# Expert blocks with gathers three blocks ahead, buffers reloaded behind their conversion, and activation splits on ScalarE and VectorE

## The chip, the cores and the metric

The kernel runs on one core of a Trainium2 chip. The metric is the device time of one execution in microseconds, the median of several runs. TensorE (PE), VectorE (DVE), ScalarE (ACT), GpSimd (POOL) and SyncE (SP) each take their own instructions in order; SP issues nearly all DMAs, POOL the indirect ones (gathers and scatters by a table of indices).

## What is computed

Three stages on 4 sequences of 768 tokens, with 384 features:

```
# 1. attention with a decaying state, 8 heads of 48
for t in range(768):
    cur = outer(u * k[t], v[t])
    y[t] = r[t] @ (state + cur)
    state = w[t][:, None] * state + outer(k[t], v[t])
# 2. dense feed-forward, 384 -> 2048 -> 384, on the 3072 tokens
h = x @ w_in
x = where(h > 0, h, exp(min(h, 0)) - 1) @ w_out
# 3. top-1 mixture of 8 experts, 384 -> 1024 -> 384
logits = x @ w_gate + modality_bias[modality_id]
e = argmax(logits); gate = softmax(logits)[e]
out = gate * (maximum(x @ w1[e], 0) @ w2[e])
```

Inputs and outputs are float32.

## The kernel before

TensorE works in float16. Every operand is held as two float16 numbers, a high half and a low half (the rest that the high half leaves), and a product is three matmuls: high by high, high by low, low by high. Making a low half is a subtraction over the whole tile, by `split` (L344) where the source is scaled, or by `lowp` (L341), whose line L342 is that subtraction on GpSimd or on VectorE:

```
def lowp(lo, f, hi, pool=True):
    (nc.gpsimd if pool else nc.vector).tensor_tensor(lo, f, hi, op=ALU.subtract)
```

**Dense groups.** The 24 tiles of 128 tokens go through the dense part in 6 groups of 4. `ffn_in` makes 16 tiles m of 9 matmuls, 512 columns each (L607); ACT's exponential (L612), two VectorE passes (L613, and L614, a maximum that reads PSUM) and an ACT copy (L615) give the high half, `lowp` the low half. `ffn_out` makes 4 token tiles of 48 matmuls, 384 columns each (L627), and `ffn_x2` stores each as two halves and transposes it by a DMA in SP's queue (L643). `logits` and `route` choose the experts. The last group has no attention beside it, but the start of the expert stage.

**Two tables.** Tokens of one expert are put together in blocks of 256. A first table (`first`, `first_b`, tag a) is made from five groups and fills the first NB = 3 blocks; a second one (`final`, `final_b`, tag b) places all that is left, and can only be made behind the last group's logits. `place_b` turns counts into index tables (idxa, idxb) by a few matmuls (L782) and nine small VectorE operations (L790 to L798). The names scr and X are the routed rows in DRAM and their source.

**Expert blocks.** There are 12 full blocks and, for these inputs, two half blocks of 128 rows, 12 and 13, counted from 0, behind branches on the numbers of blocks (`rest`, L1168 and L1173). For each block:

- `moe_gather` fetches rows by two indirect DMAs on POOL (L897) into G, one of three buffers, and SP transposes them by two DMAs (L903) into XM, also three.
- `moe_w` loads an expert's float32 weights as four quarters into four buffers (SG and, in the space of the dense weights, wi; L914, L917) and converts a quarter in two pieces, the high half by ACT (L930), the low half by VectorE (L931), into W1 and W2, two buffers each. A quarter is 768 KB.
- `moe_h` makes eight tiles of 9 matmuls, 256 columns each (128 in a half block; L939). ACT does the ReLU into mt (L945), VectorE casts it to the high half (L946), `lowp` on GpSimd makes the low half (L342).
- `moe_o` makes two token tiles of 24 matmuls, 384 columns each (one in a half block; L959): first five of the eight m for each, then the last three. VectorE scales the sum by the gate factor, which lies at the end of the gathered row in G (L966), and POOL scatters it to the output (L967).

**What sets the order.** `moe_block` issues block j's work with the loads of block j + 1 ahead of it, and the conversions of j + 1 at fixed places in it. Through `hook`, it calls the five parts of routing at ticks: the table TO gives the tick of each (`logits`, `route`, `route_b`, `final`, `final_b`), one tick for each m of `moe_h` and each step of `moe_o`, over blocks 0 and 1. A scheduler then reorders instructions within each engine, so what stands in which row is seen in the built program alone.

Of the kernel before, what the change touches and what calls it, by code (L numbers as in the profile page):

```python
# [129 lines left out]
def body(ctx, tc, r, k, v, w, u, w_in, w_out, mod, w_gate, bias, w1, w2, cst, out, dbg=None):  # L130
# [516 lines left out]
    def logits(g):
        t0, nt = GR[g]
        xt2 = xT[g]
        pt = psum("a")  # L650
        for i in range(nt):
            n = 0
            for kk in range(KD):
                for b_ in range(2):
                    for a in range(2):
                        nc.tensor.matmul(
                            pt[:, E * i:E * i + E], lhsT=xt2[:, b_ * KD + kk, 128 * i:128 * i + 128],
                            rhs=wg[:, kk, E * a:E * a + E], start=(n == 0), stop=(n == 4 * KD - 1),
                        )
                        n += 1  # L660
# [311 lines left out]
    def moe_load(j, x=True):  # L972
        e = moe_reg(j)
        moe_w(j, 0, e, 0)
        moe_w(j, 1, e, 0)
        if x:
            moe_gather(j)
        moe_w(j, 2, e, 0)
        moe_w(j, 3, e, 0)

    def moe_block(j, nxt, nt=2, x=True, hook=None, nl=True):
# [226 lines left out]
```

## Time and profile before

| | us |
|---|---|
| three runs | 894.53, 884.48, 880.47 |
| median | 884.48 |
| profiled execution | 879.89 |
| its span | 878.0 |
| TensorE busy in it | 755.0 (86%) |
| VectorE busy | 625.2 (71%) |
| GpSimd busy | 516.1 (59%) |
| ScalarE busy | 452.0 (51%) |

The profile is of one execution, the span from its first to its last instruction; 1.9 us lie outside it. The mean granted clock of TensorE is 0.955 of full speed. Lines such as L342 are lines of the kernel before. In a timeline, consecutive instructions of one kind are one row with their count, and matmuls overlap, so that a row's start minus the start of the one ahead is what it adds. In brackets stands how long the engine was idle ahead of the row and what released it: an engine with the tile and the line that it wrote.

### The profile page before, as it was taken

The numbers are of one execution on the slowest core, as the hardware profiler recorded it, in microseconds if no ns is written. First come the engines' busy times: TensorE is split into PE (matmuls) and PEld (weight loads), VectorE is DVE, ScalarE is ACT, GpSimd is POOL, SyncE is SP. The second block draws the span as 40 slices with busy tenths as digits, with TensorE's granted clock in tenths as the row PEclk, the third lists the DMA queues.
The fourth block names the chain that finished last, engine by engine and source line by source line (L and its number), as shares of the span: only waits on it lengthen the run. The fifth ranks groups of instructions, "written<-read, shape, count | busy, mean of one in ns | idle before, by whom it ended". The sixth has DMA issues, their size and how long they took to land.

```text
span 878.0 us, 17356 instructions
## 1 busy us (share of the span) xinstructions
PE 755.0 (86%) x6383; PEld 485.3 (55%) x6383; DVE 625.2 (71%) x1321; ACT 452.0 (51%) x965; POOL 516.1 (59%) x525
## 2 busy tenths in 40 slices
PE   3787575999899989998998899987997998999964
PEld 2664342665466546654665455443764765667643
DVE  5779999358965896589558951993597757776641
ACT  4675766346654565456545541462326545554431
POOL 6667778546764576467646641443255767777732
PEclk9889777999999999999999999998999999999987
DMA  9857584264366445744663321179229988888340
GB/s 219 197 127 182 124 198 101 54 107 106 75 108 113 98 78 105 114 100 77 108 110 78 46 55 37 37 255 294 64 75 349 289 243 226 252 245 263 90 160 12
DMA packets 259748, 122.23 MB, mean 139 GB/s; under 512 B 223589, under 2 KB 241162, under 8 KB 259652
## 3 DMA queue, kind: packets, MB, share of 16 engines
q1 hardware_dynamic: 255328, 110.14, 53.1%
q0 software_dynamic: 3456, 10.24, 3.5%
q8 instruction: 54, 0.88, 0.4%
q10 hardware_dynamic: 868, 0.62, 0.3%
q14 instruction: 42, 0.34, 0.1%
HBM read 81.63 MB, written 9.84 MB: 104 GB/s over the span
## 4 chain that ended last, share of the span: by engine, by line
DVE 31%; PE 23%; issue 11%; POOL 10%; DMA 9%; ACT 7%; POOLq 0%; SPq 0%; ACTq 0%; DVEq 0%
PE psf L627 16%; DVE e L613 6%; POOL gg L342 5%; DMA G<-scr,idxb 5%; DVE e L614 4%; DVE W L931 2%; DMA out_dram<-ob,idxb 2%; POOL G L897 2%; PE psf L607 2%; POOL out_dram L967 1%; DVE gg L946 1%; DMA SG<-in_moe_w_dram 1%; DVE gb L346 1%; DVE af L523 1%; DVE vb L346 1%
## 5 line engine op out<-in xcount | busy, mean ns | idle before, releaser
L607 PE MATMUL psf<-xT,wi 128*128 128x512 f16 x864 | 207.7, 393 | 30.7 <-DVE sti L293 16.0
L627 PE MATMUL psf<-wo,gg 128*128 128x384 f16 x1152 | 200.2, 330 | 10.1 <-POOL gg L342 7.4
L342 POOL TENSOR_TENSOR gg<-e,gg 128x512 f16<-128x512 f32 x96 | 116.0, 1212 | 80.1 <-ACT gg L615 72.9
L627 PEld LDWEIGHTS <-gg 128*128 128x128 f16 x1152 | 110.8, 99 | 83.4 <-POOL gg L342 8.8
L607 PEld LDWEIGHTS <-wi 128*128 128x128 f16 x864 | 84.7, 100 | 130.5 <-issue 45.2
L959 PE MATMUL psa<-W,gg 128*128 128x384 f16 x624 | 113.1, 330 | 21.3 <-POOL gg L342 17.1
L342 POOL TENSOR_TENSOR gg<-mt,gg 128x256 f16<-128x256 f32 (+1 forms) x112 | 93.3, 843 | 59.0 <-DVE gg L946 55.8
L939 PEld LDWEIGHTS <-W 128*128 128x128 f16 x1008 | 96.1, 101 | 17.4 <-issue 5.4
L959 PEld LDWEIGHTS <-gg 128*128 128x128 f16 x624 | 58.0, 98 | 70.9 <-POOL gg L342 32.0
L613 DVE TENSOR_SCALAR e<-e 128x512 f32<-128x512 f32 x96 | 83.6, 871 | 19.0 <-ACT e L612 18.0
L615 ACT ACTIVATE gg<-e 128x512 f16<-128x512 f32 x96 | 60.2, 627 | 61.5 <-DVE e L614 61.3
L946 DVE CAST gg<-mt 128x256 f16<-128x256 f32 (+1 forms) x112 | 46.9, 426 | 45.3 <-ACT mt L945 43.4
L931 DVE SCALAR_TENSOR_TENSOR W<-SG,W 128x768 f16<-128x768 f32 x56 | 55.9, 1008 | 15.2 <-ACT W L930 10.3
L612 ACT ACTIVATE e<-psf 128x512 f32<-128x512 f32 x96 | 56.3, 587 | 19.2 <-POOL gg L342 16.7
L614 DVE SCALAR_TENSOR_TENSOR e<-e,psf 128x512 f32<-128x512 f32 x96 | 65.0, 678 | 1.0
L939 PE MATMUL psf<-XM,W 128*128 128x256 f16 (+1 forms) x540 | 60.4, 269 | 5.2 <-issue 5.2
L931 DVE SCALAR_TENSOR_TENSOR W<-wi,W 128x768 f16<-128x768 f32 x56 | 57.6, 1049 | 4.4 <-ACT W L930 3.1
L930 ACT ACTIVATE W<-SG 128x768 f16<-128x768 f32 x56 | 45.8, 837 | 20.9 <-DMA SG<-in_moe_w_dram 8.8
L930 ACT ACTIVATE W<-wi 128x768 f16<-128x768 f32 x56 | 45.2, 838 | 21.0 <-PE psa L959 17.5
L945 ACT ACTIVATE mt<-psf 128x256 f32<-128x256 f32 (+1 forms) x84 | 30.4, 364 | 48.1 <-POOL gg L342 27.9
L967 POOL DMA_INDIRECT out_dram<-ob,idxb x20 | 28.5, 1424 | 33.3 <-DVE ob L966 15.3
L640 DVE SCALAR_TENSOR_TENSOR X<-psf,X 128x384 f16<-128x384 f32 x24 | 13.2, 554 | 46.6 <-ACT X L639 46.6
(312 smaller groups left out, 1413.1 us busy)
## 6 DMA issues: line engine op xcount, KB each, us to landing
SG<-in_moe_w_dram SPq DMA_DIRECT2D x28, 768.0 KB
wi<-in_moe_w_dram SPq DMA_DIRECT2D x28, 768.0 KB
stg<-in_moe_w_in_dram SPq DMA_DIRECT2D x8, 768.0 KB
stg<-in_moe_w_out_dram SPq DMA_DIRECT2D x8, 768.0 KB
scr<-X SPq DMA_DIRECT2D x6, 770.0 KB
lw<-in_w_dram SPq DMA_DIRECT2D x24, 192.0 KB
lr<-in_r_dram SPq DMA_DIRECT2D x24, 192.0 KB
lk<-in_k_dram SPq DMA_DIRECT2D x24, 192.0 KB
```

Of the source, the lines that this page charges most:

```text
L342: (nc.gpsimd if pool else nc.vector).tensor_tensor(lo, f, hi, op=ALU.subtract)
L607: nc.tensor.matmul(ph, lhsT=wi[:, a, kk, c0:c0 + 128], rhs=xg[:, b_ * KD + kk, :], start=(n == 0), stop=(n == 3 * KD - 1))
L612: nc.scalar.activation(e, ph, AF.Exp, scale=_pow2(-PH))
L613: nc.vector.tensor_scalar(e, e, 1.0, _pow2(PH), op0=ALU.min, op1=ALU.mult)
L614: nc.vector.scalar_tensor_tensor(e, e, -_pow2(PH), ph, op0=ALU.add, op1=ALU.max)
L615: nc.scalar.activation(gg[:, 0, m, 0:w_], e, AF.Copy)
L627: nc.tensor.matmul(po[:, 0:DM], lhsT=gg[:, a, m, 128 * i:128 * i + 128], rhs=wo[:, b_, m, :], start=(m == 0 and a + b_ == 0), stop=(m == N ...
L930: nc.scalar.activation(o_[:, 0], i_, AF.Copy, scale=_pow2(sc))
L931: nc.vector.scalar_tensor_tensor(o_[:, 1], i_, _pow2(sc), o_[:, 0], op0=ALU.mult, op1=ALU.subtract)
L939: nc.tensor.matmul(ph[:, 0:n_], lhsT=w_[:, a, kk, 128 * m:128 * m + 128], rhs=xm[:, b_ * KD + kk, 0:n_], start=(n == 0), stop=(n == 3 * KD ...
L946: nc.vector.tensor_copy(h2[:, 0, m, 0:n_], t_)
L959: nc.tensor.matmul(po[:, 0:DM], lhsT=h2[:, a, m, 128 * t:128 * t + 128], rhs=w_[:, b_, m, :], start=(m == 0 and a + b_ == 0), stop=(m == N ...
```

## The change

- The low half of activations in the expert blocks goes from GpSimd to VectorE, and the high half from VectorE to ACT (PSM = 0; L956 and L957 of the kernel after). In the last dense group the low half is VectorE's as well; the other groups keep GpSimd.
- Gathers are issued three blocks ahead. The transposes have a function of their own, `moe_xm`, called one block behind the gather, two blocks ahead of use. As a buffer of G is then refilled sooner, the gate factors are copied to GC, which has four buffers.
- A buffer of weights is reloaded for block j + 2 right behind its conversion for j + 1 (`conv_q`, `load_q`). One quarter is converted at m = 3, the three others in the second product. Block 13's load no longer stands behind the branch.
- On TensorE the first three tiles of the next block's `moe_h` run ahead of a block's `moe_o` (HA = 3).
- The last group's last two token tiles are transposed by TensorE with an ACT copy instead of a DMA (NPL = 2), and its logits are issued tile by tile inside its second product.
- The table of ticks becomes (0,0,7,7,20).

The diff, cut to its core:

```diff
-TO = (0,2,4,8,22)
+TO = (0,0,7,7,20)
+HA = 3
+NPL = 2
-PSM = 1
+PSM = 0
...
-        lowp(gg[:, 1, m, 0:w_], e, gg[:, 0, m, 0:w_], PSF)
+        lowp(gg[:, 1, m, 0:w_], e, gg[:, 0, m, 0:w_], g < len(GR) - 1)
...
-        nc.sync.dma_start_transpose(out=xT[g][:, :, 128 * i:128 * i + 128], in_=x2)
+        transp(xT[g][:, :, 128 * i:128 * i + 128], x2, g == len(GR) - 1 and i >= GR[g][1] - NPL, "a")
...
+    def moe_xm(j):
+        g_, xm = G[j % 3], XM[j % 3]
         for t in range(2):
             nc.sync.dma_start_transpose(out=xm[:, :, 128 * t:128 * t + 128], in_=g_[:, t, 0:DM].bitcast(F16))
+        nc.vector.tensor_copy(GC[j % 4], g_[:, :, DM:XR])
...
-        nc.vector.tensor_copy(h2[:, 0, m, 0:n_], t_)
+        nc.scalar.activation(h2[:, 0, m, 0:n_], t_, AF.Copy)
         lowp(h2[:, 1, m, 0:n_], t_, h2[:, 0, m, 0:n_], PSM)
...
-        nc.vector.tensor_scalar(ob, po[:, 0:DM], G[j % 3][:, t, DM:XR], None, op0=ALU.mult)
+        nc.vector.tensor_scalar(ob, po[:, 0:DM], GC[j % 4][:, t, :], None, op0=ALU.mult)
...
+    def load_q(j, q):
+        if q == 0:
+            RG[j] = moe_reg(j)
+        moe_w(j, q, RG[j], 0)
+
+    def conv_q(j, q, load=True):
+        if CV.get(j, 0) > q:
+            return
+        CV[j] = q + 1
+        moe_w(j, q, None, 1)
+        if load:
+            load_q(j + 1, q)
+
+    def moe_block(j, nt=2, hook=None, done=0, ahead=0, conv=False, load=False, x=False):
...
+        if x and j + 2 <= MINB + 1 and j not in (NB - 2, NB - 1):
+            moe_xm(j + 2)
         for m in range(NF2):
             tick()
+            if m >= done:
+                if m == max(done, 3):
+                    cv(0)
+                moe_h(j, m, 128 * nt)
+            if x and m == 5 and j >= NB - 1 and j + 3 <= MINB + 1:
+                moe_gather(j + 3)
+            if x and m == 5 and j == NB - 1:
+                moe_xm(j + 2)
+        for m in range(ahead):
+            moe_h(j + 1, m)
         for t in range(nt):
             tick()
+            cv(1 + t)
             moe_o(j, t, 0, NF2 - 3)
+        if nt == 1:
+            cv(2)
+        cv(3)
         for t in range(nt):
             tick()
             moe_o(j, t, NF2 - 3, NF2)
+        if x and j == NB - 2:
+            moe_gather(NB)
+            moe_gather(NB + 1)
+            moe_xm(NB)
...
+            if g == len(GR) - 1 and m == RC + 4:
+                moe_gather(1)
+                moe_xm(0)
+            if g == len(GR) - 1 and m == NF1 - 1:
+                moe_xm(1)
...
+            if g == len(GR) - 1 and i > 0:
+                logits_t(g, i - 1)
...
-                moe_block(j, j == MINB, 1, False)
+                moe_block(j, 1, conv=j == MINB)
```

Here cv(q) is `conv_q(j + 1, q, load)` where the block converts at all.

GpSimd's order from the last group into the blocks, before: gg<-e are the last group's low halves, gg<-mt the blocks', G and wi the gather's three buffers.

```order
L342 TENSOR_TENSOR gg<-e,gg 128x512 x15
L897 DMA G_7169<-scr,idxa 128x385 x2
L897 DMA G_7170<-scr,idxa 128x385 x2
L897 DMA wi<-scr,idxa 128x385 x2
L342 TENSOR_TENSOR gg<-e,gg 128x512
L342 TENSOR_TENSOR gg<-mt,gg 128x256 x10
L967 DMA out_dram<-ob,idxa 3072x384
```

After, from the end of attention on:

```order
L572 TENSOR_TENSOR x<-y,x 128x384
L904 DMA G_7169<-scr,idxa 128x385 x2
L904 DMA G_7170<-scr,idxa 128x385 x2
L904 DMA wi<-scr,idxa 128x385 x2
L978 DMA out_dram<-ob,idxa 3072x384 x2
L904 DMA G_7169<-scr,idxb 128x385 x2
L904 DMA G_7170<-scr,idxb 128x385 x2
L904 DMA wi<-scr,idxb 128x385 x2
```

The sixteenth low half stood behind the six gathers of the first table; now GpSimd has gathers and scatters alone, and the gathers of blocks 3 to 5 stand behind block 0's scatters.

VectorE's order at the end of the second table, before: ohcb and idfb to idxb are that table, W11 conversions of an odd block.

```order
L775 TENSOR_SCALAR ohcb_8190<-ohcb_8190,cs_66 128x912
L931 SCALAR_TENSOR_TENSOR W11_7174<-SG0_7167,W11_7174 128x3x256 x2
L931 SCALAR_TENSOR_TENSOR W11_7174<-SG1_7168,W11_7174 128x3x256
L790 TENSOR_SCALAR idfb_8448<-psa_8423 128x38
L791 TENSOR_SCALAR idfb_8448<-psa_8423 128x38
L931 SCALAR_TENSOR_TENSOR W11_7174<-SG1_7168,W11_7174 128x3x256
L792 CAST idtb_8449<-idfb_8448 128x38
L795 SCALAR_TENSOR_TENSOR idxb_8450<-idfb_8448,psa_8423 128x38
```

After, at the same place:

```order
L783 TENSOR_SCALAR ohcb_8211<-ohcb_8211,cs_66 128x912
L942 SCALAR_TENSOR_TENSOR W11_7174<-SG0_7167,W11_7174 128x3x256 x2
L798 TENSOR_SCALAR idfb_8441<-psa_8416 128x38
L799 TENSOR_SCALAR idfb_8441<-psa_8416 128x38
L800 CAST idtb_8442<-idfb_8441 128x38
L803 SCALAR_TENSOR_TENSOR idxb_8443<-idfb_8441,psa_8416 128x38
L942 SCALAR_TENSOR_TENSOR W11_7174<-SG1_7168,W11_7174 128x3x256
```

Two of the four conversion pieces between the table's counts and its indices have moved behind the first of the indices.

ACT's order in half block 12, before, from the branch on: mt are its ReLUs, W the conversions for block 13.

```order
L1173 UNCONDITIONAL_BRANCH
L945 ACTIVATE mt<-psf 128x128 x2
L945 ACTIVATE mt<-psa 128x128
L930 ACTIVATE W_7174<-SG_7167 128x3x256 x2
L945 ACTIVATE mt<-psf 128x128 x2
L930 ACTIVATE W_7174<-SG_7168 128x3x256 x2
L945 ACTIVATE mt<-psa 128x128
L945 ACTIVATE mt<-psf 128x128
L930 ACTIVATE W_7176<-wi 128x768 x2
```

After, at the same place, gg the high halves that are now ACT's:

```order
L1219 UNCONDITIONAL_BRANCH
L941 ACTIVATE W_7174<-SG_7167 128x3x256 x2
L941 ACTIVATE W_7174<-SG_7168 128x3x256 x2
L941 ACTIVATE W_7176<-wi 128x768 x4
L956 ACTIVATE mt<-psf 128x128 x2
L957 ACTIVATE gg<-mt 128x128 x2
```

All eight conversions of block 13 now stand ahead of block 12's first ReLU.

## Rows read from the trace of the kernel before

**Rows 1.** Windows, one a stage: stretch, us; PE, PEld, DVE, ACT, POOL busy; PEclk, DMA share, GB/s.

```profile
576.40:621.30 44.90, 36.33 (x249) 20.75 (x248) 22.72 (x40) 17.19 (x26) 15.78 (x10) 0.92 0.90 270
621.30:680.70 59.40, 51.52 (x406) 36.10 (x404) 49.37 (x142) 26.83 (x48) 29.64 (x32) 0.97 0.54 175
680.70:837.50 156.80, 145.46 (x1081) 103.23 (x1080) 110.08 (x157) 76.27 (x137) 112.74 (x109) 1.00 0.80 233
837.50:866.90 29.40, 20.86 (x194) 16.02 (x191) 12.49 (x26) 9.96 (x24) 11.97 (x19) 0.83 0.23 84
866.90:878.00 11.10, 0.00 (x0) 0.00 (x0) 0.62 (x1) 0.00 (x0) 1.00 (x1) 0.70 0.01 3
```

**Rows 2.** Timeline of PE, blocks 9 to 12: start, us, operation, [idle before <-releaser].

```profile
804.72 2.13 PE L939 MATMUL psf<-XM,W 128*128 128x256 f16 x18
806.69 1.15 PE L939 MATMUL psa<-XM,W 128*128 128x256 f16 x9
...
820.58 1.48 PE L959 MATMUL psa<-W,gg 128*128 128x384 f16 x8 [0.88 <-POOL gg L342]
...
829.75 7.96 PE L959 MATMUL psa<-W,gg 128*128 128x384 f16 x48
837.55 1.00 PE L939 MATMUL psf<-XM,W 128*128 128x128 f16 x15
```

**Rows 3.** Lines by form, 680 to 838: busy us, mean ns | idle before, releasers.

```profile
L342 POOL TENSOR_TENSOR gg<-mt,gg 128x256 f16<-128x256 f32 x72 | 65.8, 923 | 14.5 <-DVE gg L946 13.1 <-PE psa L959 1.2
...
L931 DVE SCALAR_TENSOR_TENSOR W<-wi,W 128x768 f16<-128x768 f32 x34 | 36.3, 1086 | 2.6 <-ACT W L930 1.3
...
L930 ACT ACTIVATE W<-wi 128x768 f16<-128x768 f32 x33 | 26.8, 839 | 15.0 <-PE psa L959 14.1
...
L945 ACT ACTIVATE mt<-psf 128x256 f32<-128x256 f32 x54 | 20.4, 378 | 17.0 <-POOL gg L342 13.7 <-PE psf L939 3.0
```

**Rows 4.** Timeline of PE, its gaps in the last group and in block 2.

```profile
602.74 17.82 PE L627 MATMUL psf<-wo,gg 128*128 128x384 f16 x91 [6.04 <-POOL gg L342]
...
673.68 7.15 PE L959 MATMUL psa<-W,gg 128*128 128x384 f16 x32 [4.32 <-POOL gg L342]
```

**Rows 5.** Timeline of POOL: a first gather, the split behind six, block 3's first gather.

```profile
589.85 1.92 POOL L897 DMA_INDIRECT G<-scr,idxa  x1 [2.44 <-DVE W L931]
...
601.52 1.16 POOL L342 TENSOR_TENSOR gg<-e,gg 128x512 f16<-128x512 f32 x1
...
663.83 1.04 POOL L897 DMA_INDIRECT G<-scr,idxb  x1 [5.08 <-DVE idtb L793]
```

**Rows 6.** Timeline of PE, half blocks 12 and 13.

```profile
843.38 0.48 PE L939 MATMUL psf<-XM,W 128*128 128x128 f16 x3 [4.82 <-issue]
...
861.80 1.17 PE L939 MATMUL psf<-XM,W 128*128 128x128 f16 x18
862.80 4.06 PE L959 MATMUL psa<-W,gg 128*128 128x384 f16 x24
```

**Rows 7.** Lines by form, whole execution: the same subtraction on DVE.

```profile
L342 DVE TENSOR_TENSOR Ab<-af,Ab 128x512 f16<-128x512 f32 x32 | 21.3, 681 | 0.5
```

**Rows 8.** Timeline of DVE, last group and the logits in block 0.

```profile
545.42 0.43 DVE L613 TENSOR_SCALAR e<-e 128x512 f32<-128x512 f32 x1 [1.49 <-ACT e L612]
...
547.82 0.93 DVE L613 TENSOR_SCALAR e<-e 128x512 f32<-128x512 f32 x1 [1.25 <-ACT e L612]
...
550.39 1.02 DVE L702 TENSOR_TENSOR oha<-eq,km 128x32 f32<-128x32 f32 x1
...
576.58 1.03 DVE L768 TENSOR_TENSOR pt<-pt,qal 128x20 f32<-128x20 f32 x1
...
578.66 0.68 DVE L614 SCALAR_TENSOR_TENSOR e<-e,psf 128x512 f32<-128x512 f32 x1
...
627.58 0.18 DVE L662 SCALAR_TENSOR_TENSOR lg<-psa,bsel 128x32 f32<-128x32 f32 x1
```

**Rows 9.** Timeline of SP: block 3's transposes, in SP's queue.

```profile
669.76 4.14 SPq L903 DMA_TRANSPOSE XM<-G  x2
```

More of the change, by code (lines that the diff above doesn't have):

```diff
@@ L68 @@
 MA = 3
-ML = 0
+HA = 3
+NPL = 2
 PSF = 1
-PSM = 1
+PSM = 0
 NK2 = 24
@@ L642, in ffn_x2, with logits_t, logits @@
         )
-        nc.sync.dma_start_transpose(out=xT[g][:, :, 128 * i:128 * i + 128], in_=x2)
+        transp(xT[g][:, :, 128 * i:128 * i + 128], x2, g == len(GR) - 1 and i >= GR[g][1] - NPL, "a")
     lgt = [None]
-    def logits(g):
-        t0, nt = GR[g]
[L649 to L660, printed above, removed]
+    LP = [None]
+    def logits_t(g, i):
+        xt2 = xT[g]
+        if i == 0:
+            LP[0] = psum("a")
+        pt = LP[0]
+        n = 0
+        for kk in range(KD):
+            for b_ in range(2):
+                for a in range(2):
+                    nc.tensor.matmul(
+                        pt[:, E * i:E * i + E], lhsT=xt2[:, b_ * KD + kk, 128 * i:128 * i + 128],
+                        rhs=wg[:, kk, E * a:E * a + E], start=(n == 0), stop=(n == 4 * KD - 1),
+                    )
+                    n += 1
+    def logits(g, done=0):
+        t0, nt = GR[g]
+        for i in range(done, nt):
+            logits_t(g, i)
+        pt = LP[0]
         lgt[0] = b2.tile([128, B, E], F32, tag="lg", name="lg")[:, 0:nt]
@@ L970, in moe_o, with moe_load @@
         )
-    def moe_load(j, x=True):
+    def moe_load(j):
         e = moe_reg(j)
[L974 to L981, printed above, removed]
+        for q in range(4):
+            moe_w(j, q, e, 0)
+    RG, CV = {}, {0: 0}
+    def load_q(j, q):
[10 more added lines that the diff above has]
+    def moe_block(j, nt=2, hook=None, done=0, ahead=0, conv=False, load=False, x=False):
         n = [0]
@@ L1105, in body @@
             W2 = [mp.tile([128, 2, NF2, DM], F16, name=f"W2{i}") for i in range(2)]
+            GC = [mp.tile([128, 2, 1], F32, name=f"GC{i}") for i in range(4)]
             H2 = [gg[:, :, NF2 * i:NF2 * i + NF2, 0:TB] for i in range(2)]
@@ L1150, in hook @@
                 f_()
-    moe_block(0, True, hook=hook)
-    MB1 = [0]
-    for j in range(1, MINB):
+    for j in range(MINB):
         if j == 1:
             hook(12)
-        moe_block(j, True, hook=(lambda n: hook(n + 13)) if j == 1 else None)
+        moe_block(
+            j, hook=hook if j == 0 else (lambda n: hook(n + 13)) if j == 1 else None, done=HA if j else 0,
+            ahead=HA if j + 1 < MINB else 0, conv=True, load=True, x=True,
+        )
         if j == NB:
@@ L1170, in rest @@
                 moe_load(j)
+                moe_gather(j)
+                moe_xm(j)
                 for q in range(4):
```

43 lines of the change are left out of this document (18 added, 25 removed).

## The prediction

> **What bounds the kernel now.** I first read the windows, one stretch per stage [rows 1]: the last group's second product takes 44.9 us, blocks 0 to 2 59.4, blocks 3 to 11 156.8, the two half blocks 29.4, the tail 11.1. What stands before 576.4 keeps its time, but for VectorE's extra work, which is costed below. Then I read TensorE's timeline in the blocks, for what its matmuls cost and where it stands still. One of 256 columns costs (806.69 − 804.72)/18 = 0.1094 us, one of 384 columns (837.55 − 829.75)/48 = 0.1625 [rows 2]. A full block is 72 of the first and 48 of the second: 7.88 + 7.80 = 15.68. Blocks 3 to 11 take 156.8/9 = 17.42 each, so 1.74 a block is lost; the largest piece is a gap of 0.88, ended by the low half on GpSimd [rows 2]. The groups of lines of that stretch show why it is late: its 72 splits take 65.8 us, 7.3 a block, 923 ns each, and TensorE makes a tile's sum every 9 × 0.1094 = 0.98 [rows 3]. So GpSimd keeps pace with nearly nothing to spare, its gathers and scatters come on top, and the last tiles of a block go through ReLU, cast and split on three engines while TensorE waits. TensorE is the floor; GpSimd sets what lies above it.
>
> Three larger gaps stand outside these blocks. In the last group TensorE waits 6.04 us before 602.74 for the last tile's low half [rows 4]. GpSimd had been held since 589.85 by the six gathers that stand in front of that split, and ran it at 601.52 [rows 5]. The 91 matmuls behind the gap took 17.82 against 91 × 0.1625 = 14.8. Before block 2's second product TensorE waits 4.32, again for GpSimd, and the 32 matmuls behind it take 7.15 against 5.2 [rows 4]. In half block 12 it stops for 4.82, with "issue" as the releaser [rows 6]: nothing that the profile names, close behind the branch, in a stage whose granted clock is 0.83 [rows 1].
>
> **Last group (576.4 to 621.3).** The low halves move from GpSimd to VectorE, 16 more at 0.681 [rows 7], and the gathers stand in front of no split any more. TensorE has 192 × 0.1625 = 31.2 of product and at most 68 narrow matmuls (36 of logits, 20 of the first table, 12 new transposes of the last two tiles). At what 128 columns cost in the half blocks, (862.80 − 861.80)/18 = 0.055 [rows 6], they are 3.7. VectorE is followed in its timeline [rows 8]. From 545.42 to the end of the thirteenth tile's maximum, 579.34, it needs 33.9; three more pairs of 0.43 + 0.68 are 3.3, sixteen splits 10.9: 593.5 if nothing else changes. Against that, some ten small rows between 550.39 and 576.58 are stretched to about 1.0 while GpSimd splits (1.02 on 32 elements, 1.03 on 20, beside 0.18 on 32), 5.3 us above their usual size together, and three waits for the exponential, 1.25 the longest, are 2.3: these can be filled. Lower end 585.9. TensorE needs the last low half at 576.4 + 47 × 0.1625 = 584.0. I take the lower end, as the stretching loses its cause: a wait of 1.9, between 0 and 9.5. VectorE's maxima also free the PSUM tiles of the first product; if they come late, the first product ends late instead, by the same few microseconds. Sum: 576.4 + 31.2 + 3.7 + 1.9 = 613.2 for block 0's start, 8.1 earlier.
>
> The Trainium skill, "SBUF — State Buffer", section "Who interferes with whom", says that VectorE and GpSimd share a port pair under an exclusive lock, and that a VectorE instruction with two SBUF inputs contends with a GpSimd one that reads SBUF. The stretched two-input rows agree with it. By that rule the end would be the lower one, 585.9, and by the serial sum 593.5; the rule speaks against the change where a two-input split on VectorE meets a scatter that GpSimd reads from SBUF.
>
> **Blocks 0 to 2 (59.4).** The second table is ordered two ticks earlier, and block 3's first three tiles now stand ahead of block 2's second product on TensorE, so block 3's rows are wanted 7.8 earlier. TensorE reaches them at 613.2 + 2 × 15.68 + 7.88 + 2.0 = 654.5 (2.0: the table's 24 narrow matmuls at 0.055, and small waits). The rows come by a chain that begins with the logits, summed at 627.58 [rows 8], 6.3 after block 0's start; I keep the 6.3: 619.5. From there to block 3's first gather it was 663.83 − 627.58 = 36.25 [rows 5], mostly on VectorE. Two conversion pieces leave the end of the chain (the order of VectorE in the section on the change) and GpSimd's splits no longer stretch it, but VectorE gets the blocks' splits: I take 4.5 off (bounds 0 and 6), so the gather stands at 651.3. From the gather to the end of its two transposes was 669.76 + 4.14 − 663.83 = 10.1 [rows 5, 9]. For landing I add 2: it lies between 0 and 6.8, the distance to block 3's first matmul at 680.7. That makes 663.4. A new wait of 8.9 (3 to 16) takes the place of the 4.32, and behind it stand block 2's second product, 7.8, and the 2.0 by which matmuls behind such a wait are slower (7.15 − 5.2). End 673.2: the stage takes 60.0 and gains nothing; it passes the 8.1 on, less 0.6.
>
> **Blocks 3 to 11 (156.8).** GpSimd's 65.8 goes. The high half becomes an ACT copy, the low half a VectorE subtraction. ACT has 8 conversions of 0.84 a block and 16 passes of 0.38 [rows 3]: 12.8. VectorE has 8 conversions of 1.09, 8 subtractions between 0.34 (half the columns of the 0.681 in rows 7) and 0.92 (GpSimd's time in rows 3), and 1.2 of small ones: 12.6 to 17.3. The upper end would be over TensorE's 15.68; the 0.681 is the same operation on the same engine, so I take 0.34. The three tiles of the next block stand where TensorE waited. DMA's share of 0.80 [rows 1] is 13.9 us a block, 0.88 of a period of 15.9. The gate copy (two elements a partition) and the transposes, one block behind their gather, cost nothing while the rows are a block early; if that cover goes, a block waits the 10.1 from above. I take 15.9, 0.2 above the floor, between 15.68 and 17.42: 143.1, end 816.3.
>
> **Half blocks (29.4) and tail (11.1).** A half block is 72 × 0.055 + 24 × 0.1625 = 7.9 (18 in 1.17 and 24 in 4.06, rows 6). The load of block 13 leaves the place behind the branch. ACT has eight conversions ahead of block 12's ReLUs (the order of ACT in the section on the change); six lie under block 11's second product, two of 0.84 remain: 1.7. With 15.8 for the two blocks and 0.8 for a start with no tile ahead that is 18.3 (bounds 16.8, with the conversions hidden, and 29.4, the stage as it was): 834.6. The tail stays: 845.7. The profiled execution stood 1.9 above its span, the median of the runs 4.6 above that: 847.6 to 852.2, and I say 850.
>
> **Rivals.** *VectorE late.* The last low half comes at 593.5, and the table's chain keeps its 36.25: 7.6 and 4.5 more, 862. For it: VectorE is already busy 49.4 of 59.4 in blocks 0 to 2 [rows 1], and gets work there. Against: the stretched rows.
> *The change doesn't do what it says.* GpSimd is only the last to arrive, and DMA, at 0.80 of the stage, or the order holds the period at 17.42: 9 × 1.52 = 13.7 more, 864. Against: GpSimd's 7.3 a block with its gathers and scatters, and the gap that names it.
> *Slower: a ring of buffers.* A reload now stands behind its conversion, a conversion behind its load. If the queue serves one lap at a time, four loads of 0.786 MB at 233 GB/s [rows 1] are 13.5, a conversion of a quarter 0.84 + 0.84 + 1.09 = 2.8 [rows 3], the transposes in the same queue 4.14 [rows 9]: 20.4 a block, 850 + 9 × 4.5 = 890. It decides above 15.9 + (884.5 − 850)/9 = 19.7 a block. Against: the other quarters load while one converts, and 233 GB/s has idle time in it.
>
> **How the numbers follow.** Forecast 0.62 (own range 840 to 858), VectorE late 0.17, period kept 0.16, ring 0.05. The range 838 to 872 holds the forecast's own range and both rivals on the same side, with some 8 above them for the bounds of the waits; the ring and the two rivals together stay outside. Two per cent, about what a measurement of this kernel can tell, is 866.8 and 902. Faster: 0.60 from the forecast, 0.11 and 0.10 from the next two, 0.81. Slower: 0.03, the ring at laps over 22. The same: 0.16.
>
> **What would show it.** Right: no split on GpSimd in the last group and the blocks; TensorE's gap in the last group's second product under 3; a wait of 3 to 16 for gathered rows before block 3's first tile; blocks 3 to 11 in 143; no gap of 4 behind the branch. Wrong: matmuls that wait in each block for VectorE's low half or for a conversion; a last group that ends after 618; a DMA share near 1.0 in blocks 3 to 11.

## The result and the profile after

The changed kernel takes 855.0 us in the median of four runs (853.07 to 857.23), against 886.2 for the kernel before in the same comparison: ratio 0.967, 95% interval 0.9611 to 0.9728, faster by about 3%. 850 was predicted, in a range of 838 to 872. The profiled execution took 853.07, its span 850.8. Ratios and intervals, here and below, are of the fast runs alone, those within 1.5% of the fastest of their kernel; medians and ranges are of all runs.

The windows of the kernel after, one a stage, with the columns of [rows 1]:

```profile
577.56:611.93 34.37, 33.25 (x256) 20.47 (x255) 19.93 (x50) 13.27 (x19) 6.42 (x6) 1.00 0.87 234
611.93:678.86 66.93, 55.74 (x438) 40.70 (x435) 50.87 (x152) 40.50 (x84) 18.88 (x16) 0.92 0.74 239
678.86:816.85 137.99, 137.99 (x1055) 103.06 (x1053) 95.30 (x161) 101.82 (x211) 33.87 (x29) 1.00 0.96 267
816.85:839.85 23.00, 18.14 (x194) 13.00 (x191) 12.49 (x26) 8.65 (x34) 2.69 (x3) 0.93 0.08 27
839.85:850.80 10.95, 0.01 (x1) 0.00 (x0) 0.62 (x1) 0.00 (x0) 0.98 (x1) 0.70 0.01 3
```

The last group's second product fell from 44.9 to 34.4, blocks 3 to 11 from 156.8 to 138.0, the half blocks from 29.4 to 23.0. Blocks 0 to 2 rose from 59.4 to 66.9. Three tiles of block 3, 27 x 0.1094 = 2.95, now lie in that stage and not in the next; without them it is 64.0, so 4.6 longer than before, and blocks 3 to 11 are 140.9, 15.66 each. In that stretch TensorE's column shows 137.99 busy of 137.99: it stands still nowhere, and the blocks run at the floor that the prediction put at 15.68.

The groups of lines of the kernel after from 678 to 817, beside [rows 3]:

```profile
L942 DVE SCALAR_TENSOR_TENSOR W<-wi,W 128x768 f16<-128x768 f32 x34 | 32.0, 953 | 6.1 <-ACT W L941 4.2 <-issue 1.7
...
L941 ACT ACTIVATE W<-wi 128x768 f16<-128x768 f32 x37 | 30.0, 835 | 11.8 <-PE psa L970 10.8
...
L343 DVE TENSOR_TENSOR gg<-mt,gg 128x256 f16<-128x256 f32 x69 | 27.1, 421 | 10.2 <-ACT gg L957 9.4 <-ACT mt L956 0.8
L957 ACT ACTIVATE gg<-mt 128x256 f16<-128x256 f32 x69 | 26.0, 412 | 0.6
```

GpSimd's 65.8 of splits are gone. The subtraction that took GpSimd 923 ns takes VectorE 421, and ACT and VectorE are still busy for less than TensorE's span.

The timelines of the kernel after between the last group and block 3, all engines in order of time:

```profile
612.16 1.58 ACT L941 ACTIVATE W<-wi 128x768 f16<-128x768 f32 x2 [5.10 <-DMA wi<-in_moe_w_dram]
614.37 1.58 ACT L941 ACTIVATE W<-wi 128x768 f16<-128x768 f32 x2 [0.63 <-DMA wi<-in_moe_w_dram]
615.85 0.47 ACT L640 ACTIVATE X<-psf 128x384 f16<-128x384 f32 x1
...
616.38 0.34 PE L425 MATMUL psa<-id,X 128*128 128x128 f16 x3 [1.89 <-ACT X L640]
...
621.78 0.18 DVE L670 SCALAR_TENSOR_TENSOR lg<-psa,bsel 128x32 f32<-128x32 f32 x1
...
648.89 1.07 PE L790 MATMUL psa<-ohcb,ohp 128*128 128x76 f16 x24 [3.90 <-DVE ohcb L783]
...
653.94 1.71 POOL L904 DMA_INDIRECT G<-scr,idxb  x1 [11.52 <-DVE idxb L803]
...
660.33 3.62 SPq L913 DMA_TRANSPOSE XM<-G  x2
...
666.19 4.00 PE L950 MATMUL psf<-XM,W 128*128 128x256 f16 x18 [4.86 <-DMA XM<-G]
669.98 1.25 PE L950 MATMUL psa<-XM,W 128*128 128x256 f16 x9
671.06 7.96 PE L970 MATMUL psa<-W,gg 128*128 128x384 f16 x48
```

ACT waits 5.10 for a weight load and makes four conversions, then the last tile's high half, whose sum was ready before 612; TensorE waits for it inside block 0, and the logits come 9.9 after block 0's start. TensorE waits 3.90 for the second table's operand, then 4.86 for block 3's rows, and block 2's second product, at 671.06, stands behind these. The 18 matmuls behind the wait for rows take 4.00 where 18 such take 2.13 elsewhere. The windows of the kernel after around them:

```profile
660.30:666.20 5.90, 1.04 (x11) 0.72 (x9) 3.39 (x6) 4.21 (x9) 3.20 (x3) 0.76 1.10 245
666.20:670.00 3.80, 3.80 (x19) 2.61 (x20) 3.80 (x8) 0.22 (x1) 2.58 (x2) 0.50 1.02 294
```

TensorE was busy for 1.04 of the 5.90 ahead of them, and they ran at a granted clock of 0.50, the lower of its two levels. Where "slower matmuls" stands below, it is this.

### The profile page after: what moved, and what is told of

The parts are those of the page before. It is cut to its first block, busy times and chain, and to the rows that moved or that the text cites. A ratio compares the mean times of both kernels' runs of the same rounds, so it can differ in the third digit from the quotient of the medians.

```text
span 850.8 us, 17360 instructions
## 1 busy us (share of the span) xinstructions
PE 752.4 (88%) x6395; PEld 492.0 (58%) x6395; DVE 607.7 (71%) x1351; ACT 488.4 (57%) x1079; POOL 394.2 (46%) x397
## 4 chain that ended last, share of the span: by engine, by line
PE 33%; DVE 28%; issue 10%; DMA 10%; ACT 5%; POOL 3%; SPq 0%; POOLq 0%; DVEq 0%; ACTq 0%
PE psf L628 15%; DVE e L614 6%; PE psa L970 6%; DMA out_dram<-ob,idxb 5%; DVE e L615 4%; PE psf L950 4%; PE psf L608 3%; DMA SG<-in_moe_w_dram 3%; PE psa L950 1%; POOL gg L343 1%; DVE gb L347 1%; DVE af L524 1%; DVE W L942 1%; DVE Ab L343 1%; DVE vb L347 1%
## 5 line engine op out<-in xcount | busy, mean ns | idle before, releaser
L628 PE MATMUL psf<-wo,gg 128*128 128x384 f16 x1152 | 197.2, 327 | 2.2 <-ACT gg L616 1.5
L628 PEld LDWEIGHTS <-gg 128*128 128x128 f16 x1152 | 110.0, 98 | 72.5 <-ACT gg L616 1.8
L343 POOL TENSOR_TENSOR gg<-e,gg 128x512 f16<-128x512 f32 x80 | 96.6, 1210 | 41.2 <-ACT gg L616 34.2
L970 PE MATMUL psa<-W,gg 128*128 128x384 f16 x624 | 106.4, 331 | 3.0 <-DVE gg L343 3.0
L970 PEld LDWEIGHTS <-gg 128*128 128x128 f16 x624 | 61.5, 99 | 43.8 <-DVE gg L343 3.5
L942 DVE SCALAR_TENSOR_TENSOR W<-SG,W 128x768 f16<-128x768 f32 x56 | 52.8, 955 | 31.7 <-ACT W L941 28.0
L941 ACT ACTIVATE W<-SG 128x768 f16<-128x768 f32 x56 | 45.9, 836 | 37.3 <-DMA SG<-in_moe_w_dram 34.1
L942 DVE SCALAR_TENSOR_TENSOR W<-wi,W 128x768 f16<-128x768 f32 x56 | 52.3, 954 | 18.6 <-ACT W L941 14.5
L978 POOL DMA_INDIRECT out_dram<-ob,idxb x20 | 22.8, 1140 | 87.0 <-DVE gg L343 29.9
L343 DVE TENSOR_TENSOR gg<-mt,gg 128x256 f16<-128x256 f32 (+1 forms) x112 | 42.1, 401 | 18.1 <-ACT gg L957 15.9
L957 ACT ACTIVATE gg<-mt 128x256 f16<-128x256 f32 (+1 forms) x112 | 40.7, 397 | 1.2
L343 POOL TENSOR_TENSOR Rt<-rkn,Rt 128x384 f16<-128x384 f32 x20 | 19.6, 980 | 42.3 <-ACT Rt L465 42.0
L956 ACT ACTIVATE mt<-psf 128x256 f32<-128x256 f32 (+1 forms) x84 | 29.2, 364 | 16.5 <-DVE gg L343 10.2
```

Of the source, the lines that this page charges most:

```text
L628: nc.tensor.matmul(po[:, 0:DM], lhsT=gg[:, a, m, 128 * i:128 * i + 128], rhs=wo[:, b_, m, :], start=(m == 0 and a + b_ == 0), stop=(m == N ...
L941: nc.scalar.activation(o_[:, 0], i_, AF.Copy, scale=_pow2(sc))
L942: nc.vector.scalar_tensor_tensor(o_[:, 1], i_, _pow2(sc), o_[:, 0], op0=ALU.mult, op1=ALU.subtract)
L957: nc.scalar.activation(h2[:, 0, m, 0:n_], t_, AF.Copy)
L970: nc.tensor.matmul(po[:, 0:DM], lhsT=h2[:, a, m, 128 * t:128 * t + 128], rhs=w_[:, b_, m, :], start=(m == 0 and a + b_ == 0), stop=(m == N ...
```

## The experiments

No kernel changes anything ahead of the last group, yet that group's second product began between 575 and 590 from profile to profile: by 580.5 where the mean granted clock of the execution was 0.938 to 0.962, from 587.6 on where it was 0.923 to 0.930. Single profiles are therefore compared by stage, from the start of that product on, in us:

| kernel | second product | blocks 0 to 11 | half blocks |
|---|---|---|---|
| before | 44.9 | 216.2 | 29.4 |
| after | 34.4 | 204.9 | 23.0 |
| after, a second profile (granted clock 0.923, the first 0.948) | 34.0 | 207.8 | 23.0 |
| before, blocks' engines (e4) | 41.7 | 200.4 | 22.4 |
| before, two engine edits (e13) | 35.0 | 196.5 | 22.4 |
| e13 and block 13 in front (e14) | 34.9 | 202.6 | 18.3 |
| after, no tiles ahead (e1) | 34.8 | 211.2 | 22.9 |
| after, low halves on GpSimd (e2) | 34.1 | 228.0 | 21.7 |
| after, both of these (e3) | 34.0 | 215.9 | 21.7 |
| after, last group on GpSimd (e5) | 43.6 | 205.5 | 23.0 |
| after, transposes by SP (e6) | 33.3 | 211.5 | 23.0 |
| after, block 3 not ahead (e9) | 34.1 | 204.8 | 22.4 |
| after, loads at a block's start (e15) | 38.5 | 205.3 | 22.3 |
| after, old ticks (e16) | 34.1 | 215.5 | 22.7 |

Two profiles of one kernel thus differ by 2.9 in blocks 0 to 11, all of it in blocks 0 to 2, and by 0.4 at most in the other stages. All kernels but before, after, e13, e14 and e9 have a single run.

### The blocks' engines alone, on the kernel before (e4)

```diff
-PSM = 1
+PSM = 0
-        nc.vector.tensor_copy(h2[:, 0, m, 0:n_], t_)
+        nc.scalar.activation(h2[:, 0, m, 0:n_], t_, AF.Copy)
```

> The kernel before, with only the engines of the blocks' halves changed: high half by an ACT copy, low half by VectorE. Theory: the gap of 0.88 a block ended by GpSimd shrinks to what a chain of 1.2 leaves, and blocks 3 to 11 fall from 156.8 to 141 to 148. Rival (order, DMA or tiles ahead needed): 153 or more, with another releaser in the same place, DMA or ACT. The wait of 6.04 in the last group stays in both, since that split is left on GpSimd.

Its windows, blocks 0 to 2 and 3 to 11:

```profile
622.15:679.88 57.73, 51.84 (x405) 37.94 (x402) 47.43 (x144) 35.59 (x73) 11.92 (x10) 0.94 0.55 166
679.88:822.50 142.62, 142.62 (x1081) 106.30 (x1081) 96.91 (x154) 99.12 (x208) 37.90 (x36) 0.99 0.93 265
```

Blocks 3 to 11 take 142.6, and TensorE stands still nowhere in them. That is the gain of this stage but for the 1.7 by which the kernel after is shorter still (140.9), without tiles ahead, gathers ahead or reloads behind conversions; e13 below, which has the same engines here, takes 140.95. The half blocks fall to 22.4 as well. The last group's wait for GpSimd stays, as expected, but at 3.80 and not 6.04.

### No tiles ahead (e1), and the low halves on GpSimd (e2, e3)

```diff
-HA = 3
+HA = 0
```

> The kernel after, without the three tiles of the next block ahead of a block's second product (HA = 0). Theory: the engines that make the halves set the period, and the tiles ahead only hide the last tile's chain. Behind the last tile stand a ReLU 0.38, a copy 0.42 and a subtraction 0.42, about 1.2 us, part of which the five first pieces of the second product cover: blocks 3 to 11 at 15.7 to 16.7 us each, between 141 and 150 in all against 138.0 + 2.95 of after, and TensorE's waits in them are ended by VectorE's low half. Rival: the tiles ahead are what brought the floor; then the period goes back to 17.0 or more, 153 to 157. The seam: block 3's first tile no longer waits ahead of block 2's second product, which gives back up to 4.9.

The timeline of TensorE, and of ACT ahead of the wait:

```profile
688.56 2.74 PE L970 MATMUL psa<-W,gg 128*128 128x384 f16 x8 [4.15 <-ACT gg L957]
...
711.48 2.13 PE L950 MATMUL psf<-wi,W 128*128 128x256 f16 x18
```

```profile
684.62 1.58 ACT L941 ACTIVATE W<-SG 128x768 f16<-128x768 f32 x2 [5.34 <-DMA SG<-in_moe_w_dram]
...
688.09 0.72 ACT L957 ACTIVATE gg<-mt 128x256 f16<-128x256 f32 x2
```

From 711.48, block 5's start, to the half blocks at 821.10 seven blocks take 109.62: 15.66 each, the same as with the tiles ahead. The sum from block 3's first tile on, 153.9 from 667.24, fell into the rival's numbers all the same: 36 matmuls of block 2's second product lie among block 3's there, 5.9, and TensorE waits 4.15, because ACT stood 5.34 at a conversion whose weights had not landed, with two copies that TensorE needed behind it. The period itself is the theory's, below its own range.

```diff
-PSM = 0
+PSM = 1
```

> The kernel after, with the blocks' low halves on GpSimd again (PSM = 1; the high half stays with ACT). Theory: GpSimd's 0.92 a split, with gathers and scatters of 1.0 to 1.5 each on top (8 x 0.92 + 4 x 1.2 = 12.2 of 15.7), is late by the pace of a tile, 0.98, whenever a gather stands between: period 17.0 to 17.5, blocks 3 to 11 at 153 or more, waits ended by GpSimd. Rival: 12.2 fits into 15.7 and the three tiles ahead hide the chain: period 15.7 to 15.9, 138 to 143.

The groups of lines of this kernel from 685 to 838:

```profile
L970 PE MATMUL psa<-W,gg 128*128 128x384 f16 x432 | 76.9, 336 | 11.3 <-POOL gg L343 11.3
L343 POOL TENSOR_TENSOR gg<-mt,gg 128x256 f16<-128x256 f32 x69 | 48.2, 712 | 15.7 <-ACT gg L957 6.3 <-PE psa L970 5.9 <-POOL gg L343 2.0
```

With all else of the change in place the blocks fall back: from 683.65 to 838.14 nine blocks less three tiles take 154.5, 17.5 a block, as before the change, with 11.3 of waits for GpSimd. The pace is not the reason here: a split took 712 ns, well under the 0.98 of a tile, so 8 of them are 5.7 a block. The splits wait in GpSimd's order. Its timeline at one of these waits, and TensorE's:

```profile
742.50 1.00 POOL L978 DMA_INDIRECT out_dram<-ob,idxb  x1 [5.13 <-DMA out_dram<-ob,idxb]
743.52 1.31 POOL L343 TENSOR_TENSOR gg<-mt,gg 128x256 f16<-128x256 f32 x2
```

```profile
744.26 6.32 PE L970 MATMUL psa<-W,gg 128*128 128x384 f16 x37 [2.08 <-POOL gg L343]
```

GpSimd stood 5.13 at a scatter, idle, with the next splits behind it. Ahead of block 3 TensorE waited 11.71 for gathered rows, and this is not GpSimd's order: the first gather by the second table stands 41.0 after block 0's start, as in after (42.0). The transposes behind it took 1.4 to 3.4 each there, 1.2 to 1.4 in after; why is open.

```diff
-HA = 3
+HA = 0
-PSM = 0
+PSM = 1
```

> The kernel after, with both undone: low halves on GpSimd and no tiles ahead. What is left of the change in the blocks is the copy on ACT, gathers three blocks ahead and reloads behind conversions. Theory (engines and tiles ahead share the gain): period 17.0 to 17.5 as before, 153 to 158. Rival (gathers and reloads bring the gain): 16.3 or less, 147 at most.

Blocks 0 to 11 take 215.9, as before the change (216.2). From block 3's first tile, 668.30, it is 157.9, with 1.3 of block 2's matmuls among them: 17.4 a block, the theory's. The copy on ACT, gathers ahead and reloads bring nothing without the low halves' engine. With the tiles ahead as well (e2) blocks 3 to 11 are no better and the whole is longer (228.0), mostly by the wait for rows. No run moves the low half alone and leaves the cast on VectorE.

### The last group on GpSimd again (e5), and the two engine edits alone (e13)

```diff
-        lowp(gg[:, 1, m, 0:w_], e, gg[:, 0, m, 0:w_], g < len(GR) - 1)
+        lowp(gg[:, 1, m, 0:w_], e, gg[:, 0, m, 0:w_], PSF)
```

> The kernel after, with the last dense group's low halves on GpSimd again (one argument of lowp). Six gathers stand in front of the sixteenth split once more. Theory (the split behind the gathers made the 6.04 of the last group): TensorE waits 4 to 7 in the last group's second product, released by GpSimd, and block 0 begins at 615 to 619, against 611.9 in after. Rival (the logits moved into the product, the transposes or the ticks brought the 9.4): block 0 begins by 613, with waits under 2.

```profile
609.51 1.00 POOL L904 DMA_INDIRECT wi<-scr,idxa  x1 [0.31 <-issue]
610.53 1.16 POOL L343 TENSOR_TENSOR gg<-e,gg 128x512 f16<-128x512 f32 x1
```

```profile
611.75 9.28 PE L628 MATMUL psf<-wo,gg 128*128 128x384 f16 x48 [4.41 <-POOL gg L343]
```

In GpSimd's timeline the sixth gather is followed by the last split, and TensorE waits 4.41 for it, with other waits of GpSimd and ACT ahead. The second product is 43.6 again, 9.2 longer than in after, against 44.9 before: this edit is nearly all of the last group's gain of 10.5. Block 0 began at 633.6, and not at 615 to 619, as the product itself began at 590.0.

```diff
-PSM = 1
+PSM = 0
-        lowp(gg[:, 1, m, 0:w_], e, gg[:, 0, m, 0:w_], PSF)
+        lowp(gg[:, 1, m, 0:w_], e, gg[:, 0, m, 0:w_], g < len(GR) - 1)
-        nc.vector.tensor_copy(h2[:, 0, m, 0:n_], t_)
+        nc.scalar.activation(h2[:, 0, m, 0:n_], t_, AF.Copy)
```

> The kernel before, with two edits of engines alone: the blocks' high half by an ACT copy and low half by VectorE, and the last dense group's low half by VectorE. None of the gathers ahead, tiles ahead, reloads behind conversions, transposes on TensorE or ticks. Theory (the engines are the whole gain): block 0 begins at 612 to 614, blocks 0 to 11 take the 200.4 that they took with the blocks' engines changed alone, the half blocks and the tail 33.5; span 845 to 849, so a little below after's 850.8, ratio to before 0.955 to 0.97. Rival (the rest of the change is worth something): 854 or more, 0.97 or above.

```profile
588.11:623.12 35.01, 32.46 (x238) 19.98 (x237) 23.43 (x52) 16.09 (x23) 7.17 (x6) 1.00 0.96 290
623.12:678.66 55.54, 51.11 (x412) 36.90 (x412) 45.45 (x141) 35.37 (x73) 10.41 (x8) 0.97 0.66 213
678.66:819.61 140.95, 140.95 (x1080) 105.72 (x1081) 99.06 (x157) 99.81 (x209) 40.89 (x37) 1.00 0.94 268
```

Three lines give 850.8 in the median (848.41 to 855.02), ratio 0.962 (0.9525 to 0.9715): the whole gain, as the full change's 0.967 lies inside this interval. Block 0 began at 623.1, not at 612 to 614, since the second product began at 588.1, and blocks 0 to 11 took 196.5, not 200.4. In its profile, from the second product to the end, it took 853.1 - 588.1 = 265.0 against 273.2 for after. The difference lies in blocks 0 to 2: 55.5 against 64.0 without the three tiles. Between single profiles this stage is not that sharp: e14 below, with the same order there, took 60.0.

### The seam at block 3: order, transposes, loads, ticks (e9, e6, e15, e16)

The seam is the place where block 3 first needs rows that the second table places.

```diff
-            j, hook=hook if j == 0 else (lambda n: hook(n + 13)) if j == 1 else None, done=HA if j else 0,
-            ahead=HA if j + 1 < MINB else 0, conv=True, load=True, x=True,
+            j, hook=hook if j == 0 else (lambda n: hook(n + 13)) if j == 1 else None, done=HA if j not in (0, NB) else 0,
+            ahead=HA if j + 1 < MINB and j + 1 != NB else 0, conv=True, load=True, x=True,
```

> The kernel after, but block 3's first three tiles stand behind block 2's second product, all others ahead as before. Theory (the order on TensorE made the wait of 4.86 for the gathered rows and the slower matmuls behind it): TensorE does the 7.8 of that product while the rows come, the wait falls under 1, and the time is 4 to 7 below after's. Rival (the rows come later, since gathers and transposes are themselves paced by block 2's work): the wait stays at 3 or more behind the product, and the time is within 2 of after's.

```profile
668.29 3.25 PE L970 MATMUL psa<-W,gg 128*128 128x384 f16 x19 [0.59 <-DVE ob L977]
...
673.65 1.47 PE L970 MATMUL psa<-W,gg 128*128 128x384 f16 x8 [0.80 <-DVE gg L343]
...
676.37 0.82 PE L970 MATMUL psa<-W,gg 128*128 128x384 f16 x4 [0.92 <-ACT gg L957]
```

The wait for rows is gone, but blocks 0 to 11 stay at 204.8, and the time at 852.3 (850.63 to 862.81; ratio 0.967, as after's). Waits of 3.4 in all for the gate-scaled sums and the halves of blocks 2, 3 and 5 took its place, with slower matmuls; after's waits of 1.89, 0.55 and 3.90 stand here too, at 2.00, 0.55 and 3.90. Neither expectation names this.

```diff
-NPL = 2
+NPL = 0
```

> The kernel after, with all the last group's transposes as DMAs in SP's queue (NPL = 0). In after TensorE waits 1.89 and 0.55 for the last tile's two halves inside block 0, as ACT makes the first of them behind four conversion pieces that waited 5.10 for a DMA. Theory A (the late halves set the logits, the transpose's engine does not): those waits of TensorE go, the logits come 1 to 5 later by the DMA's 2 and its landing, and block 3's first tile waits 5 to 9 in place of 4.86: time within 3 of after, either way. Theory B (transposes on TensorE are worth their place): the time is 4 or more above after's.

```profile
625.44 0.48 PE L658 MATMUL psa<-wg,xT 128*128 128x8 f16 x12 [3.15 <-DMA xT<-X]
...
681.54 4.00 PE L950 MATMUL psf<-XM,W 128*128 128x256 f16 x18 [4.89 <-DMA XM<-G]
```

```profile
620.90 4.73 SPq L913 DMA_TRANSPOSE wi<-wi  x2
...
627.81 2.55 SPq L420 DMA_TRANSPOSE xT<-X  x1
```

The second product is 1.1 shorter, the blocks 6.6 longer than in after's first profile and 3.7 longer than in its second. In SP's queue the last tile's transpose, 627.81, stands behind those of the gathered rows and weight loads, and the logits came 18.1 after block 0's start, not 9.9. From the second product on it took 278.6, against 273.2 and 276.0. That leans to theory B, that the transposes on TensorE are worth their place; with one run it is not shown.

```diff
-                conv_q(j + 1, q, load)
+                conv_q(j + 1, q, False)
...
+        if x:
+            moe_load(j + 1)
...
+            if j == MINB:
+                moe_load(j + 1)
...
```

The last group's conversions lose their reloads in the same way, and block 13's load stands behind the branch again (the last lines).

> The kernel after, with loads undone: the four quarters of block j + 1 are loaded at the start of block j, not behind conversions a block earlier. All else as after: tiles ahead, gathers ahead, engines, ticks. With the two engine edits alone blocks 0 to 11 took 196.5, with the whole change 204.9. Theory (the early reloads cost this: conversions stand in ACT's order ahead of other work and wait there for their DMA, and the reload of block 3's weights holds SP's queue until the table is there): 196 to 200, and no wait of TensorE for the last tile's halves on ACT in block 0. Rival (gathers or ticks cost it): 203 or more.

```profile
681.36 4.00 PE L950 MATMUL psf<-XM,W 128*128 128x256 f16 x18 [7.32 <-DMA XM<-G]
```

TensorE no longer waits for ACT's late half, but blocks 0 to 11 take 205.3, with 7.32 of waiting for rows: the reloads alone are not what the seam costs. The second product is 4.1 longer than in after, with waits of 2.11 for a transposed tile and 1.43 for block 0's rows.

```diff
-TO = (0,0,7,7,20)
+TO = (0,2,4,8,22)
```

> The kernel after, with the old ticks of the routing parts, (0,2,4,8,22). Theory (the table's matmuls stand too early in TensorE's order: a wait of 3.90 for VectorE): the 24 matmuls stand later, that wait falls below 2.5 and comes in a later place, but block 3's rows come later too, a wait of 5 to 9 there: blocks 0 to 11 at 203 to 207. Rival (ticks cost the difference to the two edits): 200 or less.

```profile
687.73 3.43 PE L950 MATMUL psf<-XM,W 128*128 128x256 f16 x18 [17.16 <-DMA XM<-G]
```

The table's wait falls to 1.80, but TensorE waits 17.16 for rows, 12.3 more than in after, and blocks 0 to 11 take 215.5, more than either expectation. Of the 12.3 the ticks explain some 4: the first gather by the second table stands 46.0 after block 0's start, not 42.0. From that gather to the first matmul it is 19.5, not 12.25, which is not explained.

What these say together: in after, e4 and e13 the first gather by the second table stands 41.6 to 42.0 after block 0's start, and the rows are there 54 to 58 after it. TensorE's own work for blocks 0 to 2 is 47. A kernel without tiles ahead has less to wait for there (0.24 in e13, 3.30 in e4) and goes on (55.5 and 57.7). With the tiles ahead block 2's second product, 7.8, stands behind the rows as well, and 66.9 is 54.3 + 3.8 + 1.1 + 7.8. That it is the order in this sum is read from the rows and not shown: e9, which changed it alone, did not bring the time back, as other waits came in. What of the rest (gathers, reloads, copies of the gate) makes up the difference to e13 stays open.

### Block 13 in front of the branch (e14), beside after again

On the kernel before, beside the two engine edits:

```diff
-        if nxt and nl:
+        if nxt and nl and j != MINB:
             moe_load(j + 1, x)
...
-            if nxt and m in (3, 5):
+            if nxt and m in (3, 5) and j != MINB:
...
+        if j == MINB - 1:
+            moe_load(MINB + 1, False)
+            moe_w(MINB + 1, 0, None, 1)
+            moe_w(MINB + 1, 1, None, 1)
```

The timelines of the kernel after in half block 12 show what this is for: TensorE waits for a low half on VectorE, which had eight conversions for block 13 in front of it, behind the branch.

```profile
819.08 1.01 PE L950 MATMUL psf<-XM,W 128*128 128x128 f16 x15 [1.90 <-issue]
...
819.11 3.56 DVE L942 SCALAR_TENSOR_TENSOR W<-SG,W 128x768 f16<-128x768 f32 x4 [1.43 <-issue]
822.59 3.55 DVE L942 SCALAR_TENSOR_TENSOR W<-wi,W 128x768 f16<-128x768 f32 x4
826.06 0.48 DVE L343 TENSOR_TENSOR gg<-mt,gg 128x128 f16<-128x128 f32 x2
...
826.40 5.54 PE L970 MATMUL psa<-W,gg 128*128 128x384 f16 x22 [2.97 <-DVE gg L343]
```

> The two engine edits on the kernel before, and block 13's load and the conversion of its first two quarters put in front of the branch, behind block 11. Theory (the stage of the two half blocks is held by what block 13's load and conversions put behind the branch): half blocks at 18 to 20 us in place of 22.4, all else as with the two edits, span 2 to 4 below theirs, and 5 to 12 below after's on the same chip in the stretch from the last group's second product on. Rival (the gap with no named releaser is the branch itself): half blocks stay at 21 to 23. A miss in another place is possible: ACT's conversions of block 13 now stand among block 11's ReLUs, and would hold them if their load is late.

```profile
815.67 0.56 PE L939 MATMUL psa<-XM,W 128*128 128x128 f16 x7 [0.86 <-issue]
...
819.57 4.11 PE L959 MATMUL psa<-W,gg 128*128 128x384 f16 x22 [0.50 <-DVE gg L342]
```

> The kernel after once more, beside the next three on one chip, so that they can be compared directly. From the start of the last group's second product to the span's end it took 273.2 before; 270 to 276 is expected again, whatever the part in front of it does.

The half blocks fall from e13's 22.4 to 18.3, and the two waits are 0.86 and 0.50. Against e13 the stop is 2.7 shorter; against after the wait for the low half is 2.5 shorter and the stop 1.0; the rest is slower matmuls. The load's place alone does not do it: e15 has it behind the branch and after in front, both with the eight conversions on VectorE behind the branch, and their half blocks take 22.3 and 23.0. No run moves the load and the two quarters' conversions one by one.

On one chip e14's six runs lay between 838.79 and 852.73 (median 847.6, ratio to before 0.9575, 0.9494 to 0.9655), after's six between 852.89 and 866.30 (856.7; 0.973, 0.9664 to 0.9795). The intervals just miss each other and the runs do not overlap, so this version is below after as well, by about 1.6%. From e13 it cannot be told apart by its time. The stretch from the second product on was 266.8, 6.4 below the 273.2 of after's first profile, within the 5 to 12 expected; the second profile, at the lower granted clock, took 276.0. It was not 2 to 4 below e13's 265.0: blocks 0 to 2 took 60.0 here and 55.5 there, though TensorE's order is the same in both kernels. Of these 4.5, block 0's first 27 matmuls make up 2.8: they ran at a granted clock of 0.50. That much one profile can differ in this stage.

## Why the prediction was right, and where its steps were off

The steps give 847.6 for the profiled execution, which took 853.07; 850 was said for the median, which was 855.0. Stage by stage:

| | predicted | measured |
|---|---|---|
| block 0's start | 613.2 | 611.9 |
| end of block 2's second product | 673.2 | 678.9 |
| half blocks' start | 816.3 | 816.9 |
| their end | 834.6 | 839.9 |
| span | 845.7 | 850.8 |

**Last group: right.** Predicted was a last low half at 585.9, the lower end, because the small rows stretched by GpSimd's splits would shrink. VectorE's timeline in after:

```profile
553.47 0.18 DVE L710 TENSOR_TENSOR oha<-eq,km 128x32 f32<-128x32 f32 x1
...
581.39 0.69 DVE L343 TENSOR_TENSOR gg<-e,gg 128x512 f16<-128x512 f32 x1
...
582.99 0.18 DVE L776 TENSOR_TENSOR pt<-pt,qal 128x20 f32<-128x20 f32 x1
```

The two operations that took 1.02 and 1.03 [rows 8] take 0.18, and the last low half ends at 582.1, earlier than TensorE needs it; the wait of 1.9 that was allowed for it did not come. The Trainium skill, "SBUF — State Buffer", section "Who interferes with whom", has VectorE's two-input operations contend with GpSimd's reads; the trace agrees. e5 shows that this edit is 9.2 of the gain of 10.5, and e13 has the gain (35.0) without the rest of the change.

**Blocks 0 to 2: the kind right, two sizes off.** The stage was to gain nothing; it lost 4.6. The chain was sized well: 32.2 from logits to gather (predicted 31.75) and 12.25 from gather to matmul (12.1). Off was "I keep the 6.3" for the logits, which came at 9.9, as the scheduler put four conversions ahead of the last tile's half on ACT, and one of them waited for its DMA; and TensorE's arrival, 661.3 in place of 654.5, for its own waits of 1.89, 0.55 and 3.90 and the slower matmuls behind them were not in the 2.0. TensorE came 6.8 late and the rows 2.8, so the wait for rows was 4.86, not 8.9: inside its range of 3 to 16 by two errors that partly cancel. Also, the three tiles ahead, 2.95, were counted in blocks 3 to 11 alone; that moves time between the two stages and leaves the sum.

**Blocks 3 to 11: right in size, and in the cause by e4.** 15.9 was predicted, 15.66 measured. The sentence that GpSimd "keeps pace with nearly nothing to spare" put the pace first and the gathers and scatters on top; e2, with 712 ns a split, shows that the order behind scatters does the same harm with time to spare. In the kernel before, GpSimd's timeline has both:

```profile
752.64 1.70 POOL L967 DMA_INDIRECT out_dram<-ob,idxb  x1 [1.63 <-DVE ob L966]
...
759.16 1.31 POOL L342 TENSOR_TENSOR gg<-mt,gg 128x256 f16<-128x256 f32 x2
```

Two scatters and two gathers fill 752.64 to 759.16 ahead of this block's first splits, and its eight splits then take until 768.46, 1.16 each with their waits for the cast, more than the 0.98 of a tile. Which of the two weighs more there no run shows. VectorE's 69 subtractions in the blocks of after took 414 to 446 ns each, several of them while GpSimd issued a scatter of 1.0 or more, so none was held for the length of one. And "the three tiles of the next block stand where TensorE waited" gave them a part that they don't have: e1, e4 and e13 reach the floor without them.

**Half blocks: mis-sized.** The term was 1.7 for two ACT conversions behind block 11. ACT had indeed done its conversions by 817.9. VectorE's eight, 7.1 behind the branch, were not in the step: a wait of 2.97, 2.0 more by slower matmuls behind it (5.54 for 22 against 3.6; the granted clock from 826.4 to 832.0 was 0.70), and "issue" was 1.90. That is 6.9 in place of the 1.7 and the 0.8 for a start, and the stage was 4.7 longer than predicted. (The lower bound there, 15.8 and 0.8, is 16.6, not 16.8.)

**The rivals.** VectorE was not late in the last group. The period did not keep 17.42. DMA's share rose to 0.96, which the prediction had among its signs of being wrong; the period was at the floor all the same, so that sign was none. The ring needed more than 19.7 a block; it was 15.66.

The forecast was thus near for the right reasons in the two large terms. Its errors partly cancel, which is luck: block 0 came 1.3 earlier than said and blocks 3 to 11 took 2.2 less, while blocks 0 to 2 (64.0 without the three tiles, against 60.0) and the half blocks took 8.7 more, for waits that the change added in its own order and slower matmuls behind them. The sum was 5.1 short.

## What to carry to other kernels

When an engine with several kinds of work is the last to arrive, move the work that the matmuls wait for, and measure that alone: here three lines gave the whole gain, and the rearrangement around it none that could be measured. Compare by stage and by period rather than by sum, as one stall at a seam hides a stage that is at its floor (e1). A conversion that a scheduler puts early in an in-order engine waits there for its DMA with everything behind it; follow every engine through a branch, not the one that seems fuller.

## What was not expected of the hardware

VectorE's conversions out of wi took 1086 ns before [rows 3], 1010 in e2, where GpSimd still made the low halves, and 953 in after, where it made none. A conversion has two inputs, so this fits the rule that the explanation of the last group names from the Trainium skill. GpSimd's own subtraction, 923 ns before, took 712 in e2, where the cast on VectorE, an operation with one input, had gone to ACT; why is open. No run here took the two engines apart by themselves.

In half block 12 the stop with no named releaser, 4.82 before [rows 6], was 3.56 in e13, 1.90 in after and 0.86 in e14. Block 13's load stands behind the branch in the first two and in front of it in the others, but its place is not what decides: in e15 it stands behind the branch and the stop is 1.90. There SP issued it 14 to 19 ahead of the half block, as in after, and in e13 5 to 6. While TensorE stood, the DMA engines were busy for 0.78 of the time in e13, 0.28 in after and e15, 0.47 in e14, and 0.00 in e2, where the stop was 0.18. So the long stops go with a load that is still moving; what the stop is, no run shows.
